# One TensorE operation for a pair's local scores and the value products two pairs back, in an attention and feed-forward kernel

## The chip, the cores and the metric

The kernel runs on one core of a Trainium2 chip. The metric is device time in microseconds, the median of several runs. TensorE multiplies, VectorE (DVE), ScalarE (ACT) and GpSimd (POOL) work on the results, SyncE (SP) issues most DMAs. TensorE writes into PSUM, which has eight banks here, each a 128x512 fp32 tile.

## What is computed

For each of 8 batches and 8 heads there are 512 local and 32 global tokens of 64 values. A global query attends to all keys, a local query to the 32 global keys and to the local keys within 32 places. The outcome, 4352 rows of 512, goes through a feed-forward stage with 2048 hidden values.

```python
s_g = scale * np.matmul(q_g, k_all.transpose(0, 1, 3, 2))
out_g = np.matmul(sm(s_g), v_all)
mask = np.abs(pos[:, None] - pos[None, :]) <= window          # window = 32
s_ll = np.where(mask, s_ll, -1000000000.0)
s_l = np.concatenate([s_lg, s_ll], axis=-1)
out_l = np.matmul(sm(s_l), np.concatenate([v_g, v_l], axis=2))
...
h = x @ w_in                      # x: all rows, heads side by side
g = h - np.tanh(h)
return (g @ w_out).astype(np.float32)
```

## The kernel before

The work is cut into 32 pairs of heads (four pairs are a batch) and into feed-forward chunks: one for the local rows of each batch (16 steps), and one for all global rows (8 steps). Factors of the feed-forward are split into a high and a low part, so a step has three passes of 128x512 products for the hidden values (L1219, and L1245 for the first steps) and three for the output (L1282). Between them tanh (ACT, L1227), a subtraction (DVE, L1230) and a split (L364, L1236) make the gates; the subtraction gives the hidden bank free.

From pair 4 on `attention(j)` registers a pair's operations. Keys and queries are turned by DVE (L697, L709). `add_band_scores` multiplies queries by their band of keys: 64 products of tile shape 64x32 (L730), four windows of 32 queries in four tiles for two heads. `add_band` then takes the peak (DVE, L1132), the exponential (ACT, L1137), the inverse and the scaling (POOL, L1146), and turns the probabilities into `sq` (L1152). From pair 8 on (`OWN`) `add_squares` writes them to a buffer `moved` in HBM and reads them back, shuffled, into `win_t`; `add_values` loads the values into `win_v`; `Quad.add_halves` computes the global scores of two pairs (L972), and `add_global_turn` transposes their probabilities into `win_g` (L793, L795). `add_products` multiplies values by probabilities: 128 products of tile shape 128x32 (L830; before pair 8 another form, L814), after which the result is split into `x_hi` and `x_lo` (L364, L853) and the global part is added to `xg` (L856, L858). `x_hi` and `x_lo` are the feed-forward's input, in two buffers by the parity of the batch. A pair's two products accumulators come from banks 0 to 2, as do its two score banks; hidden products use banks 0 to 3, outputs banks 4 to 7.

The order of the instructions is not that of the code. `Order.add` registers an operation with a planned length for each engine that may do it, a due time, what it reads and writes, and which banks it takes and frees. The operations are registered in program order, which sets what depends on what. `Order.run` then places them one by one, the one that can start first by the plan, with due times and penalties from `CFG` as further weights; it models the cost of a change between kinds of TensorE work (`mode`) and TensorE's clock, and puts in idle products (`filler`, L1509) where it sees a gap in the first 72 us. What it places is issued in that order on each engine. Nothing is decided at run time; engines wait on semaphores.

In the main loop (L1456) attention of a pair is registered with two steps of the feed-forward chunk of the batch before for each head.

Of the kernel before, what the change touches and what calls it, by code (L numbers as in the profile page):

```python
# [16 lines left out]
P = 128  # L17
D = 64
# [199 lines left out]
def kernel(ctx, tc, q_l, k_l, v_l, q_g, k_g, v_g, w_in, w_out, out):  # L218
# [112 lines left out]
    def bank(shape, j, dt=F32):  # L331
# [6 lines left out]
        elif len(shape) == 4:  # L338
# [4 lines left out]
    CFG = dict(a_g=-0.566, a_kg=24.4216, a_ph=0.3207, a_qs=43.4596, a_w=-0.4573, a_wn=-0.6947, a_xg=108.5443, d_g=87.2943, d_kg=23.5203,  # L343
               d_ph=18.5528, d_qh=26.732, d_qs=-0.9935, d_tg=16.3922, d_tp=57.2085, d_w=43.5209, d_wn=-1.8713, d_xg=150, d_y=-0.0857, gfirst=0,
               ho=3599.1413, hs=1711.7838, lag=-2743.2391, last=391.1946, newb=2, p0=1263.9358, pen=10.0147, penp=61.4861, s_g=56.2393,
               s_w=85.9437, step=3500.4207, step1=198.8413, lag0=-9000, hs0=705.0869, tol=0.001288688, wd0=2072.8053, wsp=-307.5092,
               xw=0.001164419, o_ld0=5073.2589, o_tn0=4454.6911, o_tg0=5044.1219, o_s0=-8594.4578, o_sp0=-1339.9745, o_t0=-5282.6239,
               o_vl0=2624.907, o_pv0=-3989.2919, wsp1=-320.7983, ho0=9000, mw=0.2623584, o_h0=-4234.6628, hp=1193.2928, bp0=7069.0075,
               bp1=-6408.65, bp2=-7528.1709, bp3=-6088.4094, p_w=67.7869, p_kg=-4.4561, mv=1.956352e-06, kd=3.585987e-05, a_sq=8.5297,
               o_gb=6802.0497, o_kl2=-7165.644, o_ql2=6972.8003, o_kt2=-7765.5577, o_qt2=-6584.9024, o_l2=-5555.4049, o_lp2=5773.8073,  # L350
               o_g2=-8484.5394, o_tg2=7874.021, o_sq2=-7916.1399, o_vl2=6980.5421, o_pv2=2749.9064, o_kl1=7985.5493, o_ql1=5604.582, o_kt1=1045.25,
               o_qt1=-3384.56, o_l1=-8976.828, o_lp1=3720.6536, o_g1=-1762.8493, o_tg1=2051.1483, o_sq1=5175.2084, o_vl1=-8947.435, o_pv1=583.2461,
               o_g0=-7214.8888, p_bd=26.0534)
# [12 lines left out]
    def either(n, kind, psum=False):  # L366

        a, d = CFG.get("a_" + kind, 0.0), CFG.get("d_" + kind, PEN if psum else 0.0)
        if psum:
            return [("A", (n + 190) / 1200, a), ("D", (n + 151) / 960, d)]  # L370
        p = [("P", 0.17 + n * 0.00192, CFG["p_" + kind])] if "p_" + kind in CFG else []
        return [("D", (n / 2 + 148) / 960, d, True), ("A", (n + 230) / 1200, a)] + p
# [23 lines left out]
    def add_weights(n):  # L396
# [52 lines left out]
        if WIDE:  # L449
            add(("A", 0.655), rebias, due, r=keys, w=keys + [("up", u)])  # L450
            add(("D", 0.42), low, due, r=keys, w=keys, lock=True)
# [48 lines left out]
    class Pair:  # L500
# [76 lines left out]
        def add_transpose(self):  # L577
# [19 lines left out]
            add([("A", 0.6, 0.0), ("D", 0.65, CFG.get("d_tg", PEN))], store, due + 0.3, r=[tg], w=["hg0", "hg1"], free=[(tg, 1)])  # L597
# [66 lines left out]
        def add_norms(self, p):  # L664
# [10 lines left out]
            add(("D", 0.37), inverse, n[0][1] - 0.5, r=[x[3] for x in n], w=[x[2] for x in n])  # L675
# [37 lines left out]
        def add_band_scores(self, *ranges):  # L713
# [4 lines left out]
            def mm(tiles):  # L718
                def fn(e, tags):
# [14 lines left out]
            for j, tiles in enumerate(ranges):  # L734
# [6 lines left out]
        def add_squares(self):  # L741
# [26 lines left out]

            if self.j >= OWN:
                add(("S", 0.6), write, self.due(self.C["o_sq"]), r=self.sqk, w=[("sd", self.u)], xfer=2.4)  # L770
                for i, ks in enumerate(((0, 3), (1, 2))):
# [617 lines left out]
    def attention(j):  # L1389
# [16 lines left out]
        if j % 2 == 0:  # L1406
            x.add_values()
# [138 lines left out]
```

## Time and profile before

| | |
|---|---|
| median of 3 runs | 911.08 us (910.80 to 911.83) |
| profiled execution | 911.43 us, its span 909.5 us |
| TensorE busy | 893.2 us, 98% of the span |
| DVE, ACT, POOL busy | 499.2, 363.5, 347.4 us (55, 40, 38%) |
| chain that ended last | 88% TensorE: 39% each L1219 and L1282, 4% L830, 3% L730 |
| granted clock | 0.995 on average |

The span runs from the first to the last instruction. The busy time of TensorE counts matrix products; weight loads run beside them in a row of their own (PEld). Products overlap, so the length of a group is best taken from the start of one group to the start of the next.

### The profile page before, as it was taken

To read this page: it belongs to the slowest core of one execution; us is meant where nothing else is said; L and a number is where in the kernel's file an instruction comes from. 1 tells how busy PE (TensorE), PEld (TensorE's weight loads), DVE (VectorE), ACT (ScalarE), POOL (GpSimd) and SP (SyncE) were. 2 spreads that over 40 slices of the span, in tenths; PEclk is the share of its full clock that TensorE was granted. 3 is DMA by queue.
4 is the path that set the end of the run, shared out by engine and by line. 5 is a ranking of instruction groups with operands and counts; after the bars stand their busy time and mean duration, and the time that the engine had idled before them with its cause. 6 is when DMAs were issued, how large, how long until landed. Compare 5 with 4: busy or idle time off the path is not lost.

```text
span 909.5 us, 23414 instructions
## 1 busy us (share of the span) xinstructions
PE 893.2 (98%) x9101; PEld 719.4 (79%) x9101; DVE 499.2 (55%) x1829; ACT 363.5 (40%) x1024; POOL 347.4 (38%) x506
## 2 busy tenths in 40 slices
PE   8999899999999999999999999999999999999998
PEld 5678678788878878788878788787888788888896
DVE  6898878836648364746557374746566461211211
ACT  5886555523334343333344343433333331222221
POOL 5576675423333333333334333333333331222221
PEclk9999999999999999999999999999999999999999
DMA  9776674755546344645545443644555321100100
GB/s 203 189 189 184 189 185 110 181 117 115 119 97 163 79 99 103 157 111 120 120 117 142 100 100 87 161 105 110 117 137 133 94 66 30 47 1 1 45 2 23
DMA packets 286958, 101.13 MB, mean 111 GB/s; under 512 B 254848, under 2 KB 277376, under 8 KB 286848
## 3 DMA queue, kind: packets, MB, share of 16 engines
q1 hardware_dynamic: 284800, 98.53, 44.4%
q8 instruction: 71, 1.16, 0.5%
q10 hardware_dynamic: 2048, 1.11, 0.4%
q14 instruction: 39, 0.32, 0.1%
HBM read 76.01 MB, written 21.50 MB: 107 GB/s over the span
## 4 chain that ended last, share of the span: by engine, by line
PE 88%; DVE 5%; DMA 2%; ACT 1%; SPq 1%; POOL 1%; issue 1%; ACTq 0%; DVEq 0%
PE bank L1219 39%; PE bank L1282 39%; PE bank L830 4%; PE bank L730 3%; DVE sq L438 1%; PE bank L814 1%; PE bank L972 1%; DMA first_q<-in_moe_w_out_dram 1%; PE bank L656 1%; PE bank L1030 1%; SPq L686 1%; DMA raw<-in_q_l_dram 0%; DMA wraw<-in_moe_w_in_dram 0%; DMA turned<-in_v_l_dram 0%; DVE t L1230 0%
## 5 line engine op out<-in xcount | busy, mean ns | idle before, releaser
L1236 POOL TENSOR_TENSOR gates<-t,gates 128x512 fp32r<-128x512 f32 x136 | 175.3, 1289 | 390.4 <-PE bank L1282 294.1
L1282 PE MATMUL bank<-w_out_hi,gates 128*128 128x512 f32 x1088 | 296.8, 392 | 2.4 <-ACT gates L364 1.5
L1282 PEld LDWEIGHTS bank<-w_out_hi,gates 128*128 128x128 f32 x1088 | 202.7, 188 | 47.1 <-ACT gates L364 2.2
L1230 DVE TENSOR_TENSOR t<-bank,t 128x512 f32<-128x512 f32 x136 | 93.6, 689 | 234.9 <-ACT t L1227 233.8
L1227 ACT ACTIVATE t<-bank 128x512 f32<-128x512 f32 x136 | 81.2, 597 | 273.2 <-PE bank L1219 270.0
L1282 PE MATMUL bank<-w_out_lo,gates 128*128 128x512 f32 x544 | 150.7, 391 | 0.0
L364 ACT CAST gates<-t 128x512 fp32r<-128x512 f32 x136 | 84.2, 619 | 133.6 <-PE bank L1282 83.6
L1219 PE MATMUL bank<-x_hi,w_in_hi 128*128 128x512 f32 x432 | 124.6, 404 | 0.0
L1282 PEld LDWEIGHTS bank<-w_out_lo,gates 128*128 128x128 f32 x544 | 102.0, 188 | 21.7 <-issue 0.2
L1219 PE MATMUL bank<-x_lo,w_in_hi 128*128 128x512 f32 x432 | 118.9, 391 | 0.0
L1219 PE MATMUL bank<-x_hi,w_in_lo 128*128 128x512 f32 x432 | 118.4, 390 | 0.0
L1146 POOL TENSOR_SCALAR prob<-prob,stats 128x128 f32<-128x128 f32 x224 | 82.8, 387 | 57.1 <-DVE stats L1142 56.6
L1137 ACT ACTIVATE prob<-prob,stats 128x128 f32<-128x128 f32 x224 | 86.9, 390 | 34.2 <-DVE stats L1132 34.2
L1219 PEld LDWEIGHTS bank<-x_lo,w_in_hi 128*128 128x128 f32 x432 | 81.4, 189 | 17.9 <-issue 0.2
L1219 PEld LDWEIGHTS bank<-x_hi,w_in_lo 128*128 128x128 f32 x432 | 81.0, 188 | 17.8
L1219 PEld LDWEIGHTS bank<-x_hi,w_in_hi 128*128 128x128 f32 x432 | 78.0, 189 | 20.5 <-issue 4.0
L793 DVE STREAM_TRANSPOSE turned<-pg 32x96 f32<-32x96 f32 x288 | 77.7, 270 | 4.3
L1132 DVE CUSTOM_DVE_ANT_0 prob<-bank,band 128x128 f32<-128x128 f32 x224 | 50.6, 283 | 38.4 <-PE bank L730 37.8
L1152 DVE STREAM_TRANSPOSE sq<-prob 128x512 f32<-128x512 f32 x50 | 35.3, 710 | 13.3 <-POOL prob L1146 11.6
L1137 ACT ACTIVATION_READ_ACCUMULATOR prob<-prob,stats 128x1 f32 x224 | 42.1, 188 | 0.0
L830 PEld LDWEIGHTS bank<-turned 128*32 128x32 f32 x3072 | 33.1, 111 | 8.5 <-DVE stats L1142 6.7
L853 DVE TENSOR_TENSOR x_lo<-bank,x_hi 128x256 fp32r<-128x256 f32 x56 | 23.4, 419 | 29.1 <-ACT x_hi L364 26.6
(161 smaller groups left out, 916.7 us busy)
## 6 DMA issues: line engine op xcount, KB each, us to landing
moved<-sq SPq DMA_DIRECT2D x24, 512.0 KB, 3.9
turned<-in_v_l_dram SPq DMA_DIRECT2D x23, 512.0 KB, 5.5
turned<-in_v_l_dram SPq DMA_DIRECT2D x32, 256.0 KB, 3.2
out_dram<-wraw SPq DMA_DIRECT2D x32, 256.0 KB, 2.4
rawkq<-in_q_l_dram SPq DMA_DIRECT2D x112, 64.0 KB, 2.3
rawkq<-in_k_l_dram SPq DMA_DIRECT2D x112, 64.0 KB, 2.3
turned<-moved SPq DMA_DIRECT2D x48, 128.0 KB, 2.7
turned<-moved SPq DMA_DIRECT2D x96, 64.0 KB, 2.3
```

What stands on the lines that cost most here:

```text
L364: (nc.scalar.copy if e == "A" else eng[e].tensor_copy)(dst, src)
L793: nc.vector.transpose(win_g[G * g:G * g + G, a.two, 3 * x:3 * x + 3], view(pgh[r, a.two, G * (j + x):G * (j + x) + 1], [(3 * G, 3), (1, G)]))
L830: m = nc.tensor.matmul(y, win_v[:, NW * a.two + w, G * d:G * d + G], x, start=n == 0, stop=n == 7, skip_group_check=True)
L1132: nc.vector.tensor_tensor_reduce(out=x[:, t], in0=self.scores[:, t], in1=bands[0 if t == 0 else 2 if t == NT - 1 else 1], scale=-0.125, sc ...
L1137: nc.scalar.activation(x[:, t], x[:, t], AF.Exp, bias=self.st[:, t:t + 1], scale=-1.0, accum_out=self.st[:, 4 + t:5 + t])
L1146: nc.gpsimd.tensor_scalar(x[:, t], x[:, t], self.st[:, 8 + t:9 + t], 1.0, op0=ALU.mult, op1=ALU.mult)
L1152: nc.vector.transpose(z[:, :, self.two].rearrange("p n t c -> p t n c"), x[:, :, k * n * G:(k + 1) * n * G].rearrange("p t (n c) -> p t n ...
L1219: nc.tensor.matmul(self.h[s][:, j * n:(j + 1) * n], w[:, cc, f * P:(f + 1) * P], self.x()[xi](cc)[:, :n], start=part == 0 and cc == 0 and ...
L1227: nc.scalar.activation(tt_[q], self.h[s], AF.Tanh)
L1230: nc.vector.tensor_sub(tt_[q], self.h.pop(s), tt_[q])
L1236: eng[e].tensor_sub(gg[q][1], tt_[q].rearrange("p (k c) -> p k c", k=4), f32(gg[q][0]))
L1282: nc.tensor.matmul(self.acc[tt], g[:, j * nt + tt], low_out(f) if wi else w_out_hi[:, f], start=s == 0 and k == 1, stop=last and k == 3 * ...
```

## The change

From pair 10 on (`late = j >= OWN + 2`) the local scores of pair j and the value products of pair j - 2 are registered as one TensorE operation (`both`), scores first. It takes four banks out of 0 to 3. Its planned length is the sum of the two with 0.127 between them. The DMAs of `sent`, for which the products wait, are tied to the first score product. To make room, values, reading of the squares and transposes of the global probabilities of pair j - 1 are registered behind the joint operation of pair j; the squares' write stays with its pair. The last two pairs' products stay by themselves. The feed-forward steps are registered four heads later from batch 3's heads on. The very last copy out of a bank is cut into two halves, on DVE and ACT. Planned lengths are changed to measured ones, and all weights in `CFG` are new, so that the whole order is another.

```diff
-        def add_band_scores(self, *ranges):
+        def add_band_scores(self, *ranges, then=None):
...
-                                nc.tensor.matmul(box["s"][a.two][G * c:G * c + G, t], query()[r, t * P + G * c:t * P + G * c + G],
-                                                 kw()[r, at:at + SQ], start=True, stop=True)
+                                m = nc.tensor.matmul(box["s"][a.two][G * c:G * c + G, t], query()[r, t * P + G * c:t * P + G * c + G],
+                                                     kw()[r, at:at + SQ], start=True, stop=True)
+                                if then and t == c == a.two == 0:
+                                    for x_ in then.sent:
+                                        tc.add_manual_dep(m.ins, x_, AFTER)
...
+            if then:
+                then.add_products(0, 1, lead=(mm(range(NT)), [f"kw{u}", f"kg{u}", "hk0"], s, self.due(self.C["o_l"])))
+            for j, tiles in enumerate(() if then else ranges):
...
+            if self.j >= OWN and part != 1:
+                add(("S", 0.45), write, self.due(self.C["o_sq"]), r=self.sqk, w=[("sd", self.u)], xfer=2.4)
+            if self.j >= OWN and part != 0:
+                for i, ks in enumerate(((0, 3), (1, 2))):
+                    add(("S", 0.9 + 1.0 * i), read(ks), self.due(self.C["o_sq"] + 1 + i), r=[("sd", self.u)], w=[("tq", 2 * i), ("tq", 2 * i + 1)],
+                        res=["h00", "h10", "h01", "h11"], xfer=1.5)
...
-                            if w == a.two == d == 0:
+                            if w == a.two == d == 0 and not lead:
...
+            if lead:
+                def both(e, tags):
+                    lead[0](e, tags)
+                    mm_windows(e, tags)
+
+                add(("T", 0.888 + 0.127 + 1.35), both, lead[3], r=reads + lead[1], w=list(o.values()) + lead[2], res=[k + (0,) for p in halves for k in x[p]] + over + ["p00", "p10"],
+                    alloc=[(y, "h") for y in lead[2] + list(o.values())], rows=0.85, ldw=0.027, tail=0.027, mode=5)
+            else:
+                add(("T", 1.35 if new else 2.1), mm_windows if new else mm, due, r=reads, w=list(o.values()), res=[k + (0,) for p in halves for k in x[p]] + over,
+                    alloc=[(o[p], self.tag) for p in halves], rows=0.9, ldw=0.027 if new else 0.053, tail=0.027 if new else 0.107, mode=5 if new else 4)
...
+                    if self.final and tt == nt - 1:
+                        def half(lo):
+                            def fn(e, _, tt=tt, key=key):
+                                copy(e, wraw[key[1]][:, lo:lo + DM // 2], self.acc[tt][:, lo:lo + DM // 2])
+                            return fn
+
+                        add(("D", 0.42), half(DM // 2), due + 0.5, r=[acc], w=[key + ("b",)], res=[key], free=[(acc, 2)])
+                        add(("A", 0.37), half(0), due + 0.5, r=[acc], w=[key], free=[(acc, 2)])
+                    else:
+                        add(either(512, "y", True), out_copy, due + 0.5, r=[acc], w=[key], free=[(acc, 1)])
...
+        late = j >= OWN + 2
         if j % 2:
             quad = Quad(j // 2)
             quad.add_scores()
-            pairs[j - 1].add_global_turn()
-            pairs[j - 1].add_products(0, 1)
+            if not late:
+                pairs[j - 1].add_global_turn()
+            if j < OWN:
+                pairs[j - 1].add_products(0, 1)
         x.add_queries()
-        x.add_band_scores(*(range(2), range(2, NT)))
+        x.add_band_scores(*(range(2), range(2, NT)), then=pairs[j - 2] if late else None)
         if j + 1 < NH // 2:
             if (j + 1) % (H // 2) == 0:
                 add_globals((j + 1) // (H // 2))
             pairs[j + 1].add_raw()
-        if j % 2 == 0:
+        if late:
+            pairs[j - 1].add_values()
+            pairs[j - 1].add_squares(1)
+            pairs[j - 1].add_global_turn()
+            x.add_squares(0)
+        elif j > OWN:
+            x.add_squares(0)
+        else:
+            if j % 2 == 0:
+                x.add_values()
+            x.add_squares()
+            if j % 2:
+                x.add_values()
+                x.add_global_turn()
+                x.add_products(0, 1)
+        if j + 1 == NH // 2:
+            pairs[j - 1].add_products(0, 1)
             x.add_values()
-        x.add_squares()
-        if j % 2:
-            x.add_values()
+            x.add_squares(1)
             x.add_global_turn()
             x.add_products(0, 1)
...
-    for i in range(NH):
-        if i >= 2 * PLAIN:
-            if i % 2 == 0:
-                attention(i // 2)
-        elif i % 2 == 0:
-            first_attention(i // 2)
-        b, h = i // H, i % H
-        if b < 2:
+    for i in range(NH + 4):
+        if i < NH and i % 2 == 0:
+            (attention if i >= 2 * PLAIN else first_attention)(i // 2)
+        if i // H < 2:
             while wn < min(len(pieces), (len(pieces) * (i + 1)) // (2 * H - 2)):
                 add_weights(wn)
                 wn += 1
-        if b > 0:
+        k = i if i < 3 * H else max(i - 4, 3 * H - 1)
+        b, h = k // H, k % H
+        if b > 0 and (i < 3 * H or k >= 3 * H):
```

The remaining hunks of the diff replace planned lengths (band peak 1.16 to 0.95, quad peak 1.5 to 2.05, global turn 1.35 to 1.65, and the like), add `lock=True` to two small DVE operations, and replace every number of `CFG`.

## Rows read from the trace of the kernel before

**Rows 1.** Busy time by stretches; columns: stretch, length, each engine's busy time, PEclk, DMA share.
```profile
0.00:180.00 180.00, 167.84 (x1338) 128.95 (x1339) 147.53 (x520) 116.54 (x331) 110.35 (x161) 0.98 0.70 179
180.00:905.00 725.00, 725.00 (x7763) 590.46 (x7763) 351.02 (x1308) 246.92 (x695) 237.10 (x346) 1.00 0.39 94
```

**Rows 2.** TensorE's timeline around one S and one P visit; columns: start us, us, what.
```profile
480.94 1.07 PE L1282 MATMUL bank<-w_out_lo,gates 128*128 128x512 f32 x4
481.85 1.07 PE L1282 MATMUL bank<-w_out_hi,gates 128*128 128x512 f32 x4
482.85 1.16 PE L730 MATMUL bank<-hl,hi 64*32 64x128 f32 x64
483.94 1.19 PE L1219 MATMUL bank<-x_hi,w_in_hi 128*128 128x512 f32 x4
484.97 1.08 PE L1219 MATMUL bank<-x_lo,w_in_hi 128*128 128x512 f32 x4
...
488.62 1.07 PE L1282 MATMUL bank<-w_out_hi,gates 128*128 128x512 f32 x4
489.62 1.54 PE L830 MATMUL bank<-turned 128*32 128x64 f32 x128
491.08 1.20 PE L1219 MATMUL bank<-x_hi,w_in_hi 128*128 128x512 f32 x4
```

**Rows 3.** TensorE's longest single wait, by what it waited for.
```profile
PE bank L730 <- DVE xg L856: 2.0, 1, 2.0
```

**Rows 4.** Busy time by stretches of 3.4 us, the two with the clock low.
```profile
20.40:23.80 3.40, 3.40 (x18) 2.54 (x17) 1.13 (x7) 2.03 (x6) 2.50 (x2) 0.51 0.79 178
108.80:112.20 3.40, 3.40 (x67) 2.63 (x68) 3.16 (x17) 2.52 (x10) 2.44 (x2) 0.56 0.68 197
```

**Rows 5.** TensorE's timeline early: L814 behind L656, and behind L730.
```profile
23.94 2.24 PE L814 MATMUL bank<-turned 128*64 128x160 f32 x32
26.11 0.51 PE L587 MATMUL bank<-idr,pg 64*128 64x64 f32 x5
...
51.09 1.16 PE L730 MATMUL bank<-kw,hi 64*32 64x128 f32 x64
52.18 2.24 PE L814 MATMUL bank<-turned 128*64 128x160 f32 x32
54.35 0.50 PE L1245 MATMUL bank<-x_hi,w_in_hi 128*128 128x512 f32 x1
```

**Rows 6.** Timeline, tanh and subtraction: a usual one, and the latest one.
```profile
461.31 0.60 ACT L1227 ACTIVATE t<-bank 128x512 f32<-128x512 f32 x1 [1.05 <-PE bank L1219]
...
461.94 0.69 DVE L1230 TENSOR_TENSOR t<-bank,t 128x512 f32<-128x512 f32 x1 [0.99 <-ACT t L1227]
...
681.90 1.66 DVE L793 STREAM_TRANSPOSE turned<-pg 32x96 f32<-32x96 f32 x6
...
682.53 0.59 ACT L1227 ACTIVATE t<-bank 128x512 f32<-128x512 f32 x1
...
685.71 0.69 DVE L1230 TENSOR_TENSOR t<-bank,t 128x512 f32<-128x512 f32 x1
```

**Rows 7.** DVE's timeline behind the value products of Rows 2.
```profile
490.95 0.42 DVE L853 TENSOR_TENSOR x_lo<-bank,x_hi 128x256 fp32r<-128x256 f32 x1 [1.34 <-ACT x_hi L364]
491.29 0.18 DVE L858 COPY xg<-bank 128x32 f32<-128x32 f32 x1
...
491.94 0.18 DVE L856 TENSOR_TENSOR xg<-bank,xg 128x32 f32<-128x32 f32 x1
```

**Rows 8.** TensorE's timeline: S of pair 9, P of pair 11, S of pair 13.
```profile
173.21 1.16 PE L730 MATMUL bank<-hl,hi 64*32 64x128 f32 x64
...
261.70 1.54 PE L830 MATMUL bank<-turned 128*32 128x64 f32 x128
...
280.65 1.16 PE L730 MATMUL bank<-hl,hi 64*32 64x128 f32 x64
```

**Rows 9.** Timeline at the end: the last copy out of a bank.
```profile
905.44 0.69 DVE L364 COPY wraw<-bank 128x512 f32<-128x512 f32 x1 [0.68 <-PE bank L1282]
```

More of the change, by code (lines that the diff above doesn't have):

```diff
@@ L596, in add_transpose @@
             add(("T", 0.42), mm, due, r=[f"pg{u}"], w=[tg], res=["hg0", "hg1"], alloc=[(tg, self.tag)], rows=0.5, mode=1)
-            add([("A", 0.6, 0.0), ("D", 0.65, CFG.get("d_tg", PEN))], store, due + 0.3, r=[tg], w=["hg0", "hg1"], free=[(tg, 1)])
+            add([("A", 0.48, 0.0), ("D", 0.65, CFG.get("d_tg", PEN))], store, due + 0.3, r=[tg], w=["hg0", "hg1"], free=[(tg, 1)])
         def add_values(self):
@@ L674, in add_norms @@
             n = [a.norms for a in self.heads]
[L675 removed]
+            add(("D", 0.37), inverse, n[0][1] - 0.5, r=[x[3] for x in n], w=[x[2] for x in n], lock=True)
             for norm, due, st, x in n:
@@ L796, in turn, with add_products @@
                         self.sent.append(x_.ins.name)
-                add(("D", 1.35 if self.j >= OWN else 1.75), turn, self.due(self.C["o_tg"]), r=["pg0"], w=[f"hg{a.two}"])
-        def add_products(self, *halves):
+                add(("D", 1.65 if self.j >= OWN else 1.6), turn, self.due(self.C["o_tg"]), r=["pg0"], w=[f"hg{a.two}"])
+        def add_products(self, *halves, lead=None):
             o = {p: (f"o{p}", "pair", self.j) for p in halves}
@@ L867, in add_products @@
             reads = [a.k(n) for a in self.heads for n in [f"h{p}" for p in halves] + ["hg", "vh"]] + [("tq", c) for c in range(4)]
-            add(("T", 1.35 if new else 2.1), mm_windows if new else mm, due, r=reads, w=list(o.values()), res=[k + (0,) for p in halves for k in x[p]] + over,
-                alloc=[(o[p], self.tag) for p in halves], rows=0.9, ldw=0.027 if new else 0.053, tail=0.027 if new else 0.107, mode=5 if new else 4)
+            if lead:
[7 more added lines that the diff above has]
+                    alloc=[(o[p], self.tag) for p in halves], rows=0.9, ldw=0.027 if new else 0.053, tail=0.027 if new else 0.107, mode=5 if new else 4)
             for p in halves:
@@ L872, in add_products @@
                 add(either(256, "ph", True), high(p), due + 0.5, r=[o[p]], w=[k + (0,) for k in x[p]])
-                add(("D", 0.55 if new else 0.65), rest(p), due + 1, r=[o[p]] + [k + (0,) for k in x[p]], w=[k + (1,) for k in x[p]] + xg_, free=[(o[p], 1)])
+                add(("D", 0.55 if new else 0.73), rest(p), due + 1, r=[o[p]] + [k + (0,) for k in x[p]], w=[k + (1,) for k in x[p]] + xg_, free=[(o[p], 1)])
     def add_globals(b):
@@ L1009, in add_halves @@
             pool = self.pairs[0].tag
-            add(("T", 0.5), mm, due(0), r=reads, w=[sg], res=all_, alloc=[(sg, pool), (sh, pool)], ldw=0.027, tail=0.027, rows=0.8, mode=3)
-            add(("D", 1.5), peak, due(1), r=[sg, ("mask", 1), "of"], w=all_ + [st], free=[(sg, 1), (sh, 1)])
-            add(("A", 0.95), exp, due(1.5), r=[st], w=all_)
-            add(("D", 0.65), inverse, due(2), r=["pg0"], w=[st])
-            add(("P", 1.45), norm, due(2.5), r=[st], w=all_)
+            add(("T", 0.53), mm, due(0), r=reads, w=[sg], res=all_, alloc=[(sg, pool), (sh, pool)], ldw=0.027, tail=0.027, rows=0.8, mode=3)
+            add(("D", 2.05), peak, due(1), r=[sg, ("mask", 1), "of"], w=all_ + [st], free=[(sg, 1), (sh, 1)])
+            add(("A", 1.15), exp, due(1.5), r=[st], w=all_)
+            add(("D", 1.1), inverse, due(2), r=["pg0"], w=[st])
+            add(("P", 1.25), norm, due(2.5), r=[st], w=all_)
         def add_scores(self):
@@ L1156, in d @@
                 return self.due(self.C["o_l"] + self.C["o_lp"] + off)
-            add(("D", 1.16), peak, d(1), r=[s] + [("band", j) for j in range(3)], w=[p, st], free=[(s, 1)])
-            add(("A", 1.6), exp, d(1.5), r=[st], w=[p])
-            add(("D", 0.33), inverse, d(2), r=[p], w=[st])
-            add(("P", 1.5), norm, d(2.5), r=[st], w=[p])
-            add(("D", 0.82 if pair.early else 0.69), turn, d(3), r=[p], w=pair.sqk, res=["rq1"] if pair.early else ())
+            add(("D", 0.95), peak, d(1), r=[s] + [("band", j) for j in range(3)], w=[p, st], free=[(s, 1)])
+            add(("A", 1.64), exp, d(1.5), r=[st], w=[p])
+            add(("D", 0.38), inverse, d(2), r=[p], w=[st], lock=True)
+            add(("P", 1.45), norm, d(2.5), r=[st], w=[p])
+            add(("D", 0.77 if pair.early else 0.71), turn, d(3), r=[p], w=pair.sqk, res=["rq1"] if pair.early else ())
         def transposes(self, pair, tags):
```

43 lines of the change are left out of this document (19 added, 24 removed).

## Prediction

> **What bounds the kernel now.** I read three views first. The busy time by stretches shows two regimes: from 180 to 905 us TensorE is busy for 725.00 of 725 us at the full granted clock, and from 0 to 180 us for 167.84 us, so 12.2 us of idle time lie there and none later [rows 1]. DVE, ACT and POOL are busy for 351, 247 and 237 us of the 725 [rows 1], so TensorE alone bounds the long part, and an edit is worth what it takes out of TensorE's own stream. The timeline of TensorE shows how that stream is made: groups of four 128x512 products whose starts lie 0.91 us apart, and between them visits of small products: 64 local scores (L730, called S) and 128 value products (L830, called P), each once per pair of heads [rows 2]. In 180 to 905 us no S visit lies next to a P visit; every one stands between big groups. The waits of TensorE, finally, say what the idle time of the first regime is: single waits of up to 2.0 us, the longest for DVE [rows 3], and two stretches where the granted clock is at its lower level, 1.2 GHz, for most of 3.4 us (0.51 and 0.56); the second begins right behind the longest wait [rows 4].
>
> **The switch saved, the main term.** Cost of an S visit: the group before starts at 481.85 and is due to end 0.91 later, at 482.76; S starts at 482.85, so 0.09 of entry; S lasts 1.09 to the next start; the big group behind it takes 1.03 to the next start where 0.91 is usual, so 0.12 of exit [rows 2]. The P visit: due at 489.53, starts at 489.62, 0.09 of entry, then 1.46 [rows 2]. Joined, one exit (behind S) and one entry (ahead of P) go: 0.12 + 0.09 = 0.21 us per pair. This counts the step from S straight to P at S's usual 1.09 and P's usual length. No row has that step. The nearest: S (L730) is once followed directly by the older value products (L814): start to start 51.09 to 52.18, again 1.09, and L814 then takes 2.17 to the next start, as it does elsewhere behind another small group (23.94 to 26.11) [rows 5]. So the drain that is inside the 1.09 stays and nothing is added; I take 0.21. The diff joins pairs 10 to 31, 22 of them; the last two value products stay alone. 22 x 0.21 = 4.6 us. Bounds: 0 if the step inside costs as much as the exit and entry that it replaces (the shapes are 64x32 and 128x32, where the row has 128x64); 22 x 0.09 = 2.0 if only P's entry goes and S's exit comes back in P's first loads; 22 x 0.30 = 6.6 if the inner drain, another 0.09, goes too.
>
> The Trainium skill, "TensorEngine Tiling (Array Packing)", Key Properties, says that changing the tiling mode, not just the tile, drains the engine. S and P are in different modes, so by that rule one drain per pair stays inside and four mode changes become three. Priced at the 0.09 of one entry [rows 2] the rule would give 2.0 us instead of 4.6, and 907.8 in place of the forecast; I give it a quarter of the forecast's chance, as the row of the nearest step agrees that a drain inside stays but shows no exit there [rows 5].
>
> **What the joint operation waits for.** It takes four accumulators at once, all of banks 0 to 3, which the hidden products also use; scores and products took two at a time before. So the last hidden product's bank must be free when it starts. That takes tanh and the subtraction: tanh starts at 461.31 and the subtraction ends at 462.63, 1.32 us [rows 6]; one output group of 12 products (three of 0.91, 2.7 us) covers it. In the worst row, with DVE transposing ahead of it, the subtraction ends at 686.40, 3.87 after tanh's start at 682.53 [rows 6]. Behind the operation, the first accumulator comes free at 491.47 and the second at 492.12, that is 0.39 and 1.04 us after P's end at 491.08 [rows 7]; again an output group covers it. Taken: nothing, as the order can put an output group on both sides; uncovered it costs what the second rival below says. In the queue of TensorE everything stands behind this wait.
>
> **What moves off TensorE.** The value loads, the reads of the squares and the transposes of global probabilities of a pair move to the next pair's turn; the same DMAs per pair stay on SP, where the next pair's key and query loads and the output writes stand behind them. Pair turns lie some 25 us apart (173.21 to 280.65 for four, on average 26.9 [rows 8]), and each datum now has a full turn more before its use. Cost nothing; cover gone, it would show as a wait of the joint operation on a DMA. The feed-forward steps of batches 2 to 6 are registered two pairs later: TensorE's total is the same, only the supply must not run dry (rival three).
>
> **The end.** The last copy is one DVE operation of 0.69 us behind the last product [rows 9]. Split in half between DVE and ACT it should take 0.42, which is what DVE needs for 256 columns out of a bank [rows 7]: -0.27 us. The DMAs behind it stay.
>
> **The new order and the lengths** touch TensorE only where it idles, 0 to 180 us. Bounds: better by all idle time, 12.2, and the clock's loss, about half of 3.4 us twice, 3.2: 15.4 us. Worse: one more wait like the longest, 2.0, with a slow stretch behind it, 1.5: 3.5 us. The longest wait ends on DVE [rows 3], some of whose work the old plan took as too short (a head's global transposes, planned at 1.35 with a seventh, last 1.66 us for the first six [rows 6]), and the new lengths correct part of that; I count 1.0 us, half of that wait of 2.0.
>
> **Sum.** The profiled execution took 911.43 us (span 909.5 and 1.93 around it). 911.43 - 4.6 - 0.3 - 1.0 = 905.5. The median of the runs, 911.08, lies 0.35 lower: 905.2.
>
> **Rivals.**
> 1. *The switch is not saved*: the step inside costs what exit and entry did. For it: S uses two row halves, P full columns, and no row has that pair of shapes. Against: the 1.09 in [rows 5]. Then only end and order count: 911.08 - 1.3 = 909.8.
> 2. *Banks, the slower side*: TensorE stops at the joint operation or behind it because all four banks are wanted. It decides from 0.21 us per pair on, where the saving is gone. For it: the second accumulator is free 1.04 us after P's end, the first 0.39, and one subtraction in every four pairs comes as late as the row of [rows 6]. If hidden products follow at once and wait 0.39 for the first bank in every pair, that is 22 x 0.39 = 8.6 us: 905.2 + 8.6 = 913.8. A late subtraction in every fourth, 3.87 less the cover of 2.7, would add 5 x 1.2 = 6 to that: 920 at the most. Against: an output group is nearly always at hand, since TensorE never waited for a gate after 180 us [rows 1].
> 3. *Supply, slower too*: batch 2's hidden products need pair 11's values, which now come with pair 13's scores. Before, pair 11's P ran at 261.70 while S of pair 13 ran at 280.65 [rows 8]. To keep TensorE fed, S of pairs 10 to 13 must follow S of pair 9 (173.21) within 88.5 us, 22.1 each; they took 26.9 [rows 8]. Kept at 26.9, the gap is up to 19 us: 905.2 + 19 = 924; half of it, 915. Against: DVE, which turns and reduces each pair's data, is busy for less than half of 180 to 905 us, so pairs can follow faster [rows 1].
> 4. *The new order takes half of the 15.4 us out of the start*: 905.2 + 1.0 - 7.7 = 898.5.
> 5. *The new order adds a wait of 3.5 us there*: 905.2 + 1.0 + 3.5 = 909.7.
>
> **How the numbers follow.** Forecast 905.2, with 902.5 to 908 as its own range (4.6 between 2.0 and 6.6, the order's term within 1 us): chance 0.62. Rival 1: 0.10. Rival 2: 0.09. Rival 3: 0.04. Rival 4: 0.10. Rival 5: 0.05. The range leaves out rivals 2 and 3 and the far side of rival 4: 898.5 to 910.0. A difference under 0.2%, 1.8 us, is about what a measurement can't tell from none. Faster by more: forecast and rival 4, with 0.02 of rival 1: 0.74. Same: the rest of rival 1, rival 5 and 0.01 of a mild rival 2: 0.14. Slower: 0.12.
>
> **What will show it.** Right: 22 places where L830 starts 1.09 us behind L730 with no big group between, each followed by a first big group of 1.03; TensorE still 100% busy from 180 us on; the last DVE copy at 0.42. Wrong: a step from L730 to L830 of 1.3 (rival 1); TensorE waits on DVE ahead of L730 or L1219 after 200 us (rival 2); one gap of several us between 250 and 290 us (rival 3); or the difference of the spans lying ahead of 180 us (rivals 4 and 5).

## The result, and the profile after

| | before | after |
|---|---|---|
| median of 4 runs each | 911.28 us (910.80 to 911.83) | 921.06 us (919.71 to 921.58) |
| profiled execution, its span | 911.43, 909.5 us | 919.71, 917.9 us |
| ratio after to before | | 1.0105, 95% interval 1.0087 to 1.0122 |

The change makes the kernel 1% slower. The forecast was 905.2 us, with 898.5 to 910.0 as its range: the sign was wrong. In the changed kernel the lines are S: L729, P: L836, hidden products L1233, output products L1296.

I read the waits of TensorE first. Columns: what waited on what, us in total, times, longest.

```profile
PE bank L836 <- issue: 9.4, 6, 2.2
...
PE bank L1296 <- issue: 0.8, 1, 0.8
...
PE bank L1233 <- DVE stats L1146: 0.2, 1, 0.2
```

The first line is new: six times TensorE stands still in the value products, 9.4 us in all, and no engine, bank or DMA is named. "issue" means that the profile shows nothing that it waited for. The second line shown is a seventh standstill, just behind an operation. The kernel before has no line with "issue" at all. The last line is the only wait for another engine behind 180 us: hidden products behind pair 21 wait for DVE, which reads the scores out of their bank (L1146).

The stretches that answer to [rows 1] say in which regime the time was lost (stretch, length, then PE, PEld, DVE, ACT, POOL, granted clock, DMA):

```profile
0.00:180.00 180.00, 168.62 (x1345) 129.38 (x1346) 145.31 (x529) 113.52 (x317) 108.96 (x161) 0.98 0.69 176
180.00:905.00 725.00, 714.62 (x7730) 586.49 (x7729) 343.53 (x1293) 255.22 (x710) 236.53 (x346) 1.00 0.40 95
```

TensorE is no longer busy throughout the long part: 10.4 us of idle time lie there, and the granted clock there is 1.00 as before. The start is little changed (168.62 for 167.84 us).

TensorE's timeline around the joint operation of pair 10, and of pair 12, which answers to [rows 2]:

```profile
196.75 1.16 PE L729 MATMUL bank<-kw,hi 64*32 64x128 f32 x64
197.84 1.53 PE L836 MATMUL bank<-turned 128*32 128x64 f32 x124
200.98 0.31 PE L836 MATMUL bank<-turned 128*32 128x64 f32 x4 [1.61 <-issue]
201.22 2.14 PE L1296 MATMUL bank<-w_out_hi,gates 128*128 128x512 f32 x8
...
250.18 1.16 PE L729 MATMUL bank<-kw,hi 64*32 64x128 f32 x64
251.27 1.56 PE L836 MATMUL bank<-turned 128*32 128x64 f32 x128
252.76 2.12 PE L1296 MATMUL bank<-w_out_hi,gates 128*128 128x512 f32 x8
```

Pair 12 is what was forecast: S to P 1.09, P 1.49 to the next start. In pair 10 the same operation stops after 124 of P's 128 products, and P takes 3.38 us from start to start. So it is not the beginning of the operation that waits (as it would for banks or data), but a place in the middle of a string of products that are ready. From start to start, P takes 3.38, 2.95, 3.37, 2.83, 3.89 and 3.24 us in pairs 10, 11, 18, 26, 28 and 29, and 1.47 to 1.50 in all others but pair 30 (1.68); behind pairs 21 and 23 the next products take 0.4 and 1.0 us longer. Together that is some 12.4 us: 11.0 in P and 1.4 behind it. The 0.4 behind pair 21 is where the wait for DVE lies; whether that wait or the cause found below held TensorE there, the trace does not tell.

What could stop a queue in the middle? The page's list of DMA queues has a row for the instructions themselves (packets, MB, share):

```profile
q8 instruction: 71, 1.16, 0.5%
```

71 packets of 16 KB for the 2 x 9110 instructions of TensorE (each product comes with a weight load) and a few more: one packet for every 256 or so. That the queue is TensorE's shows in the packets' times: from the first (20.72) to the last (888.31) the trace records 254 products and loads per packet. A joint operation has 384 of them (64 and 128 products, with their loads), in 2.6 us. In a big group 256 instructions take 29 us (128 products 0.227 apart). I counted TensorE's instructions from the program and laid the borders between packets over the timeline. One number, the origin of the count, was set so that pair 10 fits; then all seven standstills for "issue" in the trace (pairs 10, 11, 18, 23, 26, 28 and 29) lay on a border, the second one in or just behind the operation, and the first border lay 52 to 132 instructions behind the operation's start in all seven. In the other operations the first border lay elsewhere. That is theory A, code loading. The rivals: theory B, banks or data (which would tie the standstills to pairs, not to positions in the instruction stream), and a busy DMA.

### The profile page after: what moved, and what is told of

It reads as the page before. It is cut to its first block, busy times and chain, and to the rows that moved or that the text cites. A ratio compares the mean times of both kernels' runs of the same rounds, so it can differ in the third digit from the quotient of the medians.

```text
span 917.9 us, 23461 instructions
## 1 busy us (share of the span) xinstructions
PE 891.9 (97%) x9110; PEld 722.7 (79%) x9110; DVE 490.0 (53%) x1824; ACT 370.9 (40%) x1029; POOL 346.8 (38%) x507
## 3 DMA queue, kind: packets, MB, share of 16 engines
q8 instruction: 71, 1.16, 0.5%
q10 hardware_dynamic: 2048, 1.11, 0.5%
## 4 chain that ended last, share of the span: by engine, by line
PE 85%; DVE 6%; issue 2%; ACT 2%; DMA 2%; SPq 2%; POOL 1%; ACTq 0%; DVEq 0%
PE bank L1296 38%; PE bank L1233 36%; PE bank L836 4%; PE bank L729 3%; SPq L756 1%; DVE sq L437 1%; PE bank L820 1%; PE bank L986 1%; DVE wraw L432 1%; PE bank L655 1%; DMA first_q<-in_moe_w_out_dram 1%; DVE turned L792 1%; DMA raw<-in_q_l_dram 1%; DVE t L1244 0%; PE bank L1190 0%
## 5 line engine op out<-in xcount | busy, mean ns | idle before, releaser
L1296 PE MATMUL bank<-w_out_hi,gates 128*128 128x512 f32 x1088 | 297.0, 396 | 4.3 <-ACT gates L363 3.5
L1296 PEld LDWEIGHTS bank<-w_out_hi,gates 128*128 128x128 f32 x1088 | 202.3, 189 | 49.9 <-ACT gates L363 4.2
L1296 PE MATMUL bank<-w_out_lo,gates 128*128 128x512 f32 x544 | 151.3, 392 | 0.0
L1233 PE MATMUL bank<-x_hi,w_in_hi 128*128 128x512 f32 x432 | 119.3, 392 | 0.2 <-DVE stats L1146 0.2
L1296 PEld LDWEIGHTS bank<-w_out_lo,gates 128*128 128x128 f32 x544 | 101.8, 188 | 22.0 <-issue 0.5
L1233 PE MATMUL bank<-x_lo,w_in_hi 128*128 128x512 f32 x432 | 118.2, 389 | 0.0
L1233 PE MATMUL bank<-x_hi,w_in_lo 128*128 128x512 f32 x432 | 118.0, 389 | 0.0
L1233 PEld LDWEIGHTS bank<-x_hi,w_in_lo 128*128 128x128 f32 x432 | 81.0, 188 | 17.3
L1233 PEld LDWEIGHTS bank<-x_hi,w_in_hi 128*128 128x128 f32 x432 | 80.5, 188 | 18.0 <-issue 0.6
L1233 PEld LDWEIGHTS bank<-x_lo,w_in_hi 128*128 128x128 f32 x432 | 81.1, 188 | 17.0
L1146 DVE CUSTOM_DVE_ANT_0 prob<-bank,band 128x128 f32<-128x128 f32 x224 | 50.3, 285 | 29.0 <-PE bank L729 28.9
L836 PE MATMUL bank<-turned 128*32 128x32 f32 (+1 forms) x3072 | 38.8, 206 | 9.4 <-issue 9.4
L836 PEld LDWEIGHTS bank<-turned 128*32 128x32 f32 x3072 | 34.0, 111 | 15.3 <-issue 14.9
```

What stands on the lines that cost most here:

```text
L836: m = nc.tensor.matmul(y, win_v[:, NW * a.two + w, G * d:G * d + G], x, start=n == 0, stop=n == 7, skip_group_check=True)
L1146: nc.vector.tensor_tensor_reduce(out=x[:, t], in0=self.scores[:, t], in1=bands[0 if t == 0 else 2 if t == NT - 1 else 1], scale=-0.125, sc ...
L1233: nc.tensor.matmul(self.h[s][:, j * n:(j + 1) * n], w[:, cc, f * P:(f + 1) * P], self.x()[xi](cc)[:, :n], start=part == 0 and cc == 0 and ...
L1296: nc.tensor.matmul(self.acc[tt], g[:, j * nt + tt], low_out(f) if wi else w_out_hi[:, f], start=s == 0 and k == 1, stop=last and k == 3 * ...
```

## The experiments

Ratios are to runs of the kernel before that were taken with each set: medians 911.59 us for the first four experiments, 911.40 for the others.

**1. Shift the stream.** The same work in the same order, with every border moved by 108 instructions.

```diff
+            for _ in range(108):
+                nc.tensor.nop(hint="pad")
             for j in range(8):
                 nc.tensor.matmul(bank([P, 4, P], tags["warm"])...
```

> The changed kernel with 108 idle instructions (they compute nothing) on TensorE ahead of its warm-up products; everything behind them is as it was, so the pairs' data, banks, transfers and order are the same. Theory A, code loading: the page of the changed kernel lists 71 packets of 16 KB of instructions, and TensorE has some 18,370 instructions, one packet for every 256 or so. A joint operation has 384 (64 and 128 products, each a weight load and a product, those in fp32 counted twice), done in about 2.6 us where a big group takes 8.8 us for 256, so it is the only place at which two borders between packets can come within 3 us. In the changed kernel TensorE stands still in the joint operations of pairs 10, 11, 18, 23, 26, 28 and 29, which are those whose first border lies 52 to 132 instructions behind their start. With all borders 108 instructions earlier in the stream of work these are pairs 12, 13, 14, 15, 22 and 31, and 27 in part: theory A expects value products of 3 us and more there and of about 1.5 us in 10, 11, 18, 26, 28 and 29, some 11 us in total as before (12), and a time of 920, within 2 us. Theory B, the joint operation waits for its banks or its data: the same pairs stand still as before, and the time is 921 as well. So not the time but the places tell.

(The expectation's 8.8 us for 256 instructions of big groups is wrong; it is 29, as above.) Measured: 926.95 us (925.11 to 929.79), ratio 1.0167 (1.0140 to 1.0193) to the kernel before. All the old places are gone (P of pair 10 takes 1.49, of 28 1.47), and pairs 12, 13, 14, 15, 22 and 31 take 3.16, 2.91, 3.10, 3.29, 3.37 and 3.19; behind 27 the next group is 0.6 longer. Only pair 21 (2.01; its first border lies 31 instructions in) was not foreseen; in the changed kernel pair 16, with its first border at 31 too, took 1.50. TensorE's timeline, pairs 10 and 14, and the first row of all:

```profile
8.70 3.72 PE L1397 MATMUL bank<-gates 128*128 128x512 f32 x8 [8.70 <-issue]
...
205.57 1.16 PE L729 MATMUL bank<-kw,hi 64*32 64x128 f32 x64
206.66 1.57 PE L836 MATMUL bank<-turned 128*32 128x64 f32 x128
...
309.97 1.55 PE L836 MATMUL bank<-turned 128*32 128x64 f32 x126
312.87 0.27 PE L836 MATMUL bank<-turned 128*32 128x64 f32 x2 [1.35 <-issue]
```

Theory B falls: the pairs' data, banks and transfers are the same, and the standstills went to other pairs. The time missed its 920 for a reason beside the point: the first product starts at 8.70 instead of 1.04, so 108 idle instructions with no product to cover them cost 7.7 us, 71 ns each.

**2. Scan the position.** 938 idle instructions, spread over the operations ahead of each joint one, put the first border at 22 chosen places.

```diff
+            for _ in range(before[i]):
+                self.idle()
             if o is None:
                 self.filler(*e)
```

> The changed kernel with 938 idle instructions on TensorE, spread over the steps ahead of each joint operation so that the first border between two packets of instructions falls 118, 50, 170, 152, 146, 70, 142, 138, 134, 60, 130, 126, 110, 42, 100, 90, 80, 12, 46, 38, 34 and 24 instructions behind the start of the joint operations of pairs 10 to 31. Theory A (code loading) expects no standstill below about 30 and above about 146, and in between one that grows from 1.4 us at 50 to 2.2 at 110 and falls to 0.3 at 139, pair by pair, whichever pair it is: 22 us in total, a time of about 931. Theory B (banks or data) expects 10, 11, 18, 23, 26, 28 and 29 to stand still and no other, at about 921.

Measured: 932.53 us (one run), for 931. By position of the first border, P's excess over 1.48 and that of the group behind it in us: at 12: 0; 24: 0.4; 34: 0.3; 38: 0; 42: 0.8; 46: 1.7; 50: 2.1, and 1.5 in the group behind; 60: 1.7; 70: 1.4; 80: 1.5; 90: 1.9; 100: 1.9; 110: 1.5; 118: 1.8; 126: 1.9; 130: 1.5; 134: 0.9; 138: 0.4; 142: 0.4; 146, 152 and 170: 0. A sample from TensorE's timeline, first border at 170 (pair 12) and at 80 (pair 26), and the stretch behind the operation with its first border at 50 (pair 11):

```profile
254.87 1.57 PE L851 MATMUL bank<-turned 128*32 128x64 f32 x128
...
619.84 1.33 PE L851 MATMUL bank<-turned 128*32 128x64 f32 x104
622.43 0.45 PE L851 MATMUL bank<-turned 128*32 128x32 f32 x24 [1.26 <-issue]
```

```profile
229.30:232.90 3.60, 3.60 (x15) 2.85 (x10) 2.85 (x13) 3.46 (x17) 1.28 (x1) 0.53 0.56 127
```

The place decides, whichever pair it is, from 42 on. Below that it does not alone: 24 and 34 stood still, 38 did not (the last section has what tells them apart). The step at 130 to 146 came where expected; between 46 and 126 the excess scatters between 1.4 and 2.1 instead of rising from 1.4 to 2.2. The 1.5 us behind pair 11 are no standstill: TensorE is busy, and the granted clock was 0.53 on average over 3.6 us, mostly at its lower level of 1.2 GHz, right behind a standstill of 1.9 us.

**3. Put every border where it does no harm.** The same edit with 682 idle instructions in seven places.

> The changed kernel with 682 idle instructions on TensorE, in seven places, so that the first border between packets of instructions falls 20 to 24 or 157 to 225 instructions behind the start of every joint operation: nowhere in the stretch in which theory A (code loading) sees a standstill. Theory A expects no standstill in any of the 22, so about 12.3 us less than the changed kernel: 908.8, within 1.5; that is also the test of the prediction's main term, the switch saved, since the standstills are what hid it. Theory B (banks or data) expects the same pairs to stand still and about 921. The idle instructions themselves lie in the queue ahead of big groups; each adds a few ns where TensorE's queue runs dry, 682 of them 10 us at the most if none is covered.

Measured: 908.20 us (906.45 to 909.09), ratio 0.9955 (0.9939 to 0.9972). TensorE's row of P in the costliest groups (before the same row reads 37.0 us and no idle time), and two stretches:

```profile
L851 PE MATMUL bank<-turned 128*32 128x32 f32 (+1 forms) x3072 | 37.5, 206 | 0.0
```

```profile
0.00:180.00 180.00, 168.72 (x1349) 128.52 (x1349) 144.97 (x529) 114.19 (x320) 109.90 (x163) 0.99 0.70 177
180.00:895.00 715.00, 715.00 (x7741) 588.37 (x7740) 344.26 (x1294) 255.14 (x708) 235.67 (x344) 1.00 0.40 96
```

No standstill that the profile lists is left (P takes 1.47 to 1.54, once 1.66), TensorE is busy for 715.00 of 715 us, and the kernel is faster than both others. With 12.9 us back from idle instructions alone, the mechanism is shown. Behind big groups the idle instructions cost nothing that these rows show; at the first run's 71 ns, 682 with no cover would cost 48 us, and not the expectation's 10.

**4. Take the two halves apart again**, in the new order: the scores (parts[0]) stay, the value products (parts[1]) come behind the next TensorE operation.

```diff
+            elif hasattr(o.fn, "parts"):
+                o.fn.parts[0](e, o.args)
+                held = o
...
+            elif e == "T" and held:
+                held.fn.parts[1]("T", held.args)
+                held = None
```

> The changed kernel with the two halves of each joint operation apart again: the value products are issued behind the TensorE operation that follows the scores, everything else in the new order and with the same number of instructions. No run of 384 quick instructions is left. Theory A (code loading): no standstill behind pair 10, but the 22 switches are paid again: 921.1 - 12.3 + 4.6 = 913.4, within 2. Theory B (banks: four accumulators wanted at once): also no standstill, since the banks are taken two at a time again, so this run tells the two apart only together with the first three. Against the third run it prices the switch: 4.6 us by the prediction, 0 by its first rival.

Measured: 917.88 us (915.93 to 921.55), ratio 1.0059 (1.0039 to 1.0080). The time is 4.5 us over the expected 913.4. Six standstills stayed, 3.9 us in all, which I had not expected. Pair 11 on TensorE's timeline:

```profile
226.07 1.16 PE L741 MATMUL bank<-hl,hi 64*32 64x128 f32 x64
227.15 1.20 PE L1309 MATMUL bank<-w_out_hi,gates 128*128 128x512 f32 x4
228.28 1.09 PE L848 MATMUL bank<-turned 128*32 128x64 f32 x86
229.72 0.64 PE L848 MATMUL bank<-turned 128*32 128x32 f32 x42 [0.35 <-issue]
```

The next operation is a group of only four products; it takes 1.13 us and eight instructions, so the two borders move apart by 1.1 us and not by enough. The loss is smaller than in the changed kernel in all seven pairs: by 0.95, 0.95, 1.31, 0.4, 1.08, 0.97 and 0.57 us in pairs 10, 11, 18, 23, 26, 28 and 29, on average 0.9. So the standstill counts from the first border, not from the operation, which bears theory A out in rough size. The group in between takes 1.13 where four products take 0.91 [rows 2]: 0.22 us per pair (in every fourth pair it has three products and takes 0.90 for 0.68), 22 x 0.22 = 4.8 us, is the price of being apart. 908.2 + 4.8, and 5.2 for P (41.0 us from start to start in all, for 35.8 in the third run), is 918.2, for 917.9 measured; as the runs spread over 5.6 us, it is luck that the two lie so close.

**5. One packet more.** The third run's kernel with the value products issued twice, so that a joint operation has 640 instructions.

```diff
                     lead[0](e, tags)
                     mm_windows(e, tags)
+                    mm_windows(e, tags)
```

> The third run's kernel (e3_fix: 682 idle instructions, no standstill) with the value products of each joint operation issued twice; the second set writes the same sums over the first. A joint operation then has 640 instructions instead of 384, the extra 256 are one packet exactly, so the first borders stay at 20 to 24 and 157 to 225 instructions behind its start, and one border more lies in or just behind the operation. In the runs so far TensorE passes the second border 2.9 to 3.8 us behind the first, with one to two thirds of that time spent on products. Theory A1: only one packet is under way at a time, so every border costs some 3 us from the one before it: in the four cases of borders (24 and 20: 280 and 536; 225: 481; 157: 413) a standstill of about 1.5 us in every one of the 22 joint operations, together 33 us, and 32 for the products themselves (22 times 1.47): 908.2 + 65 = 973, within 10. Theory A2: the packets come one by one only after a long quiet stretch, or several are held ahead: the standstills stay under 0.5 us each, and the time is 908.2 + 32 = 940, within 5.

Measured: 990.93 us (one run), for 973 within 10. TensorE's waits, pair 11 on its timeline, and the stretch behind pair 18:

```profile
PE bank L851 <- issue: 41.1, 22, 2.8
```

```profile
226.90 1.16 PE L744 MATMUL bank<-hl,hi 64*32 64x128 f32 x64
227.98 1.68 PE L851 MATMUL bank<-turned 128*32 128x64 f32 x143
231.44 1.37 PE L851 MATMUL bank<-turned 128*32 128x32 f32 x113 [1.78 <-issue]
```

```profile
434.80:438.20 3.40, 3.40 (x9) 2.63 (x9) 3.26 (x13) 0.32 (x1) 1.27 (x1) 0.50 0.57 133
```

All 22 stand still, 1.4 to 2.8 us each: theory A1, and rather more than its 33 us. Of the 82.7 us over the third run, 41.1 are standstills and 32.3 the products. Behind four of the longer standstills (pairs 16, 18, 28 and 29, 2.0 to 2.4 us) the granted clock was 0.50 to 0.53 for 3.4 to 3.6 us, by these figures some 1.7 us lost each and 6.8 in all; the longest standstill (2.8, pair 12) had no such stretch behind it. Theory A2, packets held ahead, falls.

**The packets themselves.** No run was needed for this: the trace lists DMA packets of a stretch by queue. In the changed kernel's pair 10 (first border by count at 197.77, TensorE goes on at 200.98) the stretches 196.75 to 198.30 and 198.45 to 201.90 hold no packet at all on any queue; 198.30 to 198.45 and 201.90 to 202.10 hold one each:

```profile
q8 instruction: 1, 0.02, 49.4%
...
q8 instruction: 1, 0.02, 27.4%
```

So a packet of instructions is fetched 0.6 us behind the first border, with the DMA queues otherwise empty, and TensorE passes the second border 2.6 us after that; the next packet follows 1.0 us behind this. In the pairs 11, 18, 23, 26, 28 and 29 TensorE goes on 2.3 to 2.7 us behind the packet as well. Throughout this trace and those of the first two runs, packets and counted borders pair off one for one in order. In the fifth run's pair 11 the two packets lie at 228.8 and 232.6, and TensorE goes on at 231.44. A busy DMA is not needed for it: in pair 10 nothing else was moved, and in pairs 28 and 29 the DMA share from packet to work was 0.03, with 2.42 and 2.35 us between the two. It may lengthen a standstill: in pair 28, the longest, the packet started 2.31 us behind the first score, for 1.64 and 1.75 in pairs 10 and 29 with their borders at like places, and the DMA share before it was 0.53. That the load was the reason is not shown.

**6. Again, with all borders far from harm and a whole last copy.**

```diff
-    chunks[-1].final = True
```

> As the third run (idle instructions ahead of joint operations), but 779 of them, chosen so that every first border falls 183 to 251 instructions behind the start of its joint operation, and with the last copy whole again on one engine, as in the kernel before. Theory A expects no standstill; value products that took 0.05 to 0.19 us over 1.47 in a few pairs whose border lay at 20 to 24 should take 1.47 to 1.50 in all (0.4 us in total). The end: in the changed kernel's trace the two halves of the last copy ran one behind the other (0.42, then 0.37), so a whole one of 0.69 should give back 0.1 to 0.15. Expected 908.2 - 0.5 = 907.7, within 1.0. If the rest of the distance to the forecast (905.2) were left in the joint operations, nothing would come back.

Measured: 908.17 us (907.22 to 909.67), ratio 0.9964 (0.9953 to 0.9976). P takes 1.47 to 1.50 in 21 of 22 pairs (1.63 in pair 30), as expected, but the median is that of the third run: half a microsecond is less than these runs can tell. The last copies on the timeline, of the changed kernel, and of this run:

```profile
913.27 0.39 PE L1296 MATMUL bank<-w_out_hi,gates 128*128 128x512 f32 x1
913.70 0.42 DVE L363 COPY wraw<-bank 128x256 f32<-128x256 f32 x1 [6.88 <-PE bank L1296]
914.15 0.37 ACT L363 COPY wraw<-bank 128x256 f32<-128x256 f32 x1 [1.24 <-DVE wraw L363]
```

```profile
901.97 0.39 PE L1311 MATMUL bank<-w_out_hi,gates 128*128 128x512 f32 x1
902.59 0.59 ACT L378 COPY wraw<-bank 128x512 f32<-128x512 f32 x1 [0.98 <-PE bank L1311]
```

Halved, ACT's part is released by DVE's and runs behind it: the copy ends 1.25 us after the last product's start. Whole on ACT it ends after 1.21, whole on DVE in the kernel before after 1.11 (last product at 905.02, copy in [rows 9]).

**7. The old order under the new operation.** The planned lengths and the order's numbers of the kernel before; idle instructions placed anew.

```diff
-    CFG = dict(a_g=-4.4567, a_kg=34.1826, ...
+    CFG = dict(a_g=-0.566, a_kg=24.4216, ...
...
-            add(("D", 0.95), peak, d(1), ...
+            add(("D", 1.16), peak, d(1), ...
```

> The changed kernel with joint operations, but with the planned lengths and the order's numbers of the kernel before, and with 739 idle instructions placed anew so that the first borders fall 12 to 24 or 156 to 212 instructions behind the start: only the new lengths and the new order are undone. The prediction counted 1.0 us for them (between 3.5 lost and 15.4 won): 908.2 + 1.0 = 909.2. From the trace of the changed kernel, where waits in the start fell by 1.1 us but products that only keep the clock up rose by 2.9: 907 to 908. If the joint operation needs the new order to be fed in time (rivals 2 and 3 of the prediction), TensorE waits for gates or value data behind 180 us here, and the time is above 912.

Measured: 932.04 us (930.99 to 932.22), ratio 1.0222 (1.0208 to 1.0235). TensorE's waits, and the timeline of pair 13 with the DVE work that releases it (L1162 reads the scores out of their bank):

```profile
PE bank L1249 <- DVE stats L1162: 12.3, 5, 2.5
PE bank L1312 <- ACT gates L379: 5.6, 6, 1.9
```

```profile
267.82 1.54 PE L852 MATMUL bank<-turned 128*32 128x64 f32 x128
...
271.49 0.29 DVE L1162 CUSTOM_DVE_ANT_0 prob<-bank,band 128x128 f32<-128x128 f32 x1
271.70 0.42 DVE L875 TENSOR_TENSOR x_lo<-bank,x_hi 128x256 fp32r<-128x256 f32 x1
271.83 1.80 PE L1249 MATMUL bank<-x_hi,w_in_hi 128*128 128x512 f32 x4 [2.47 <-DVE stats L1162]
```

In the old order hidden products follow the joint operation in every fourth pair and wait 2.4 to 2.5 us for a bank of its scores. That is the second rival of the prediction in kind and place; the bank is that of the scores, not the accumulator that it priced at 0.39. Behind 180 us the waits come to 16.7 us (12.3 for this bank, 4.4 for gates), and five stretches of 3.4 to 3.6 us there run at a granted clock of 0.50 to 0.53, three of them within 1.2 us behind such a wait and two as close behind a wait for gates of 1.9 us. The first of them:

```profile
272.00:275.60 3.60, 3.60 (x10) 2.79 (x11) 3.45 (x15) 0.83 (x5) 0.00 (x0) 0.53 0.88 312
```

The new order, with its lengths, keeps an output group behind every joint operation and is worth 24 us (932.0 to 908.2) to this change, not the 1.0 that I had counted.

**8. Only the joining undone**, for the planner too.

```diff
-        x.add_band_scores(*(range(2), range(2, NT)), then=pairs[j - 2] if late else None)
+        x.add_band_scores(*(range(2), range(2, NT)), then=None)
+        if late:
+            pairs[j - 2].add_products(0, 1)
```

> The changed kernel with scores and value products as two operations for the planner as well (two accumulators at a time, each placed on its own, none joined), but with the new lengths, the new order's numbers, the later value products and the halved last copy: only the joining is undone. No run of 384 quick instructions is left by construction unless the plan puts the two side by side. Theory A expects no standstill, and 22 switches paid again: 908.2 + 4.8 = 913.0, within 1.5, a little above the kernel before. If the prediction's terms for order and end were right, this kernel lies 1.3 below the kernel before: 910.

Measured: 919.25 us (917.22 to 920.56), ratio 1.0082 (1.0068 to 1.0096): 6 us over the expected 913. The trace has two waits in P that I had not foreseen:

```profile
PE bank L836 <- DMA rawkq<-in_q_l_dram: 1.2, 1, 1.2
PE bank L836 <- issue: 1.1, 1, 1.1
```

The second is code loading once more: a P alone is 256 instructions, and it stopped two products before its end (at 518.26 it went on). By count a border lies 5 instructions ahead of its first product and the next 251 behind, and a packet started at 515.99, 2.27 us before TensorE went on. Some 3.4 us lie ahead of 185 us, where this kernel has 15 big products more left to do than the third run; they are not explained. The plan came from numbers that were chosen for joint operations, so this run does not price the joining; the fourth does.

## Why the prediction was wrong

- **What bounds the kernel.** Right: TensorE alone in the long part, and the loss lies in TensorE's own stream.
- **The switch, 22 x 0.21 = 4.6 us.** Right. S to P takes 1.08 to 1.09, and the price of being apart was 0.22 (fourth run). The bound of 2.0, which went by one drain more, is out. From 185 us to the last product's start TensorE takes 720.0 us before and 714.8 in the third run, which has two big products (0.23 each) fewer to do there: 4.7 less for the same work.
- **"What the joint operation waits for. Taken: nothing."** This step failed. It went through banks, data and queues, all that the profile names as a releaser, and they did hold. It left out that the instructions have to be there. The trace of before could have shown the two halves of it: the page's row of instruction packets, and 384 instructions in 2.6 us by [rows 2]. What it could not show was the price, for there no run of 384 quick instructions existed, and no wait for "issue". Measured: 12.4 us, which turns some 4.7 won into some 8 lost.
- The Trainium skill, "Runtime: NRT & Kernel Launch", Instruction fetch mechanics, says that instructions come in blocks of 16 KiB, 256 of them, that the next is fetched while the present one runs, and that crossing a border is mostly hidden. The packets of 16 KB agree. For these runs of quick instructions "hidden" does not hold (1.4 to 2.8 us per operation in the fifth run), and the measurement decides.
- **Rivals.** None was it. The second had the sign (913.8, at most 920), and its mechanism is real, but in the old order (seventh run); in the changed kernel one wait of 0.2 us is all that appears of it behind 180 us. Rival 3, supply: no such gap; P of pair 11 ran with S of pair 13 as planned, and the third run has no wait at all behind 185 us.
- **The end, -0.27.** Wrong sign: +0.14, as the halves run one behind the other.
- **The order, -1.0.** Wrong twice. In the start it shows no gain: waits of TensorE there fell from 11.8 to 10.5 us in all, but the products that only fill its queue rose from 13 to 22. And the step said that the order touches TensorE only in the start; in fact it decides what stands behind each joint operation (seventh run).
- **The sum, mended.** On the profiled spans: 909.5 - 4.8 + 12.4 + 0.14 = 917.2, for 917.9. Of the rest, 0.7, some 0.5 lies ahead of 185 us, where the changed kernel is two big products behind. On the medians the rest is 2.0, and I can't place it. Without the standstills the forecast's mechanism gives 908.2 (third run) instead of 905.2. The order's and the end's terms are 1.4 of that; the spread from run to run (906.45 to 909.09 for one kernel) can hide the rest, which no run splits up.

## What to carry to other kernels

When small, quick operations are joined to save switches, count their instructions as well as their time: on TensorE here a run of 384 within 2.6 us can cross two borders of instruction packets, and whether it stands still depends on where the first falls. Idle instructions ahead of it, under the cover of long products, move the border for nothing; the same ones with no cover cost 71 ns each. And an order of work that is set anew with a change should be weighed with the change: what stands behind the new operation decides which of its banks is waited for.

## What the runs showed of the hardware

- Packets of 256 TensorE instructions come one by one: no two start closer than 3.2 us in any of the ten traces, and TensorE goes on 2.2 to 2.9 us behind the start of the one that it needs (standstills of 0.3 us and more in P, in the changed kernel and the first, second, fourth and fifth runs). A packet's transfer takes 0.9 to 1.2 us of one DMA engine in the two shown (49.4% of 16 engines for 0.15 us, 27.4% for 0.20); what fills the rest was not found.
- A first border at 42 to 134 cost 0.8 us and more in the second run, one from 146 on nothing there. At 3 to 38 it is the start of that border's packet that tells, in the changed kernel and the first two runs: where it lay 0.55 to 2.8 us ahead of the first score, P stood still in none of ten pairs; where it lay 0.14 to 0.37 us ahead, 0.2 to 0.4 us in each of three; 0.22 us behind, 0.5 us in one. So near the low end the packet can be on its way while the big group before is still running.
- Standstills and waits can cost clock as well: behind some of 1.9 to 2.5 us (second, fifth and seventh runs) the granted clock was 0.50 to 0.53 for 3.4 to 3.6 us, with TensorE busy. Behind those of the changed kernel, up to 2.2 us, it stayed at 1.00.
- Value products alone, without scores, are open to it as well: one stood still for 1.1 us in the eighth run.
